# Gate and up of one transformer layer: paired 64-row products replaced by 128-row products in block 3, and by seven shared products for the last tiles of blocks 2 and 3

## The chip, the core and the metric

The kernel runs on one core of a Trainium2 chip. The time is device microseconds (us) of one execution. Five engines work side by side, each through its own queue of instructions in order: PE (TensorE, matrix products), DVE (VectorE), ACT (ScalarE), POOL (GpSimd) and SP (SyncE, which here only issues DMAs). An instruction waits on semaphores of other engines; whatever stands behind it on its own engine waits with it.

## The reference

One pre-LayerNorm layer on 2048 tokens of width 576: multi-query attention with 32 heads of width 18, then a bilinear feed-forward network (FFN) of width 4608.

```python
def _A_ref(x, wq, wk, wv, wo):            # H = 32, Dh = 18; one k and one v for all heads
    q = (x @ wq).reshape(B, S, H, Dh).transpose(0, 2, 1, 3)
    k, v = x @ wk, x @ wv
    p = softmax(einsum("bhqd,bkd->bhqk", q, k) * Dh ** -0.5)
    o = einsum("bhqk,bkd->bhqd", p, v)
    return o.transpose(0, 2, 1, 3).reshape(B, S, H * Dh) @ wo
def _B_ref(x, w_gate, w_up, w_down):
    return ((x @ w_gate) * (x @ w_up)) @ w_down
h = x + _A_ref(layernorm(x), ...)
out = h + _B_ref(layernorm(h), ...)
```

## The kernel before

The 2048 tokens are four blocks of 512 (NB = 4), the FFN width is 36 tiles of 128 (NF = 36). Every float32 operand is split into a rounded high part and a remainder, and a product is hi·hi + hi·lo + lo·hi. A split is a cast (on ACT or POOL, line L88) and a subtraction on DVE (L89).

**Gate and up.** The width 576 is nine chunks of 64 rows. For one tile the weight operand `ws` holds gate in rows 0 to 63 and up in rows 64 to 127, and `X` holds the normed tokens twice, in both halves. Each step is a pair of matmuls of 64 rows and 512 columns that work at the same time in the two halves of the array (L990). Nine chunks of three terms are 27 pairs per tile. Then ACT copies gate out of PSUM (`g`, L1020) and DVE multiplies by up (`hf`, L1024). A tile of weights (`wr`, 576 KB) is loaded by one DMA and split by POOL and DVE (128x1152).

**Down.** Two tiles together go through a scheme of seven products of quarters; its left operands are sums of quarters of the two `hf` (`S`, four DVE operations), split into the buffer `room`, and its right operands `wdo` are seven loads of 288 KB per pair of tiles from a DRAM copy made in block 0. These are 42 matmuls of 128 rows and 288 columns in 14 stages on three PSUM banks (L950, `down`). After each stage its bank is added to the residual `h`, eight times by DVE (L953), six times by an ACT copy and a POOL addition; a bank's next stage waits for that.

**Order.** The program is written out by one Python pass. Attention of the next block is interleaved with the FFN of the present one, so that the last attention work ends inside tile 24 of block 2. From there on PE has only FFN work ("gu" tiles, whose PSUM tile is `gu`), and the down products of a pair come after the first tile of the next pair. The attention output of block 3 is projected in five chunks; the last two (`project`, matmuls `yo`, L754, 24 and 16 of them) are put between these tiles by `run_aux`. When the last is added to `h`, DVE computes LayerNorm statistics (L103, L104, two BN_STATS and one BN_AGGR for each 128 tokens) and the reciprocal root (thirteen small operations, L113 to L124 and L791).

**Block 3's X.** In tile 35 of block 2 ACT makes the normed tokens `xh` (L801), PE transposes them (`tx`, 20 at L823), ACT casts, DVE subtracts, and eight DMAs from SBUF to SBUF fill X's second half (X<-X). The last pair of block 2 (48 matmuls, L908) stands between. Then block 3's 36 tiles run.

Of the kernel before, what the change touches and what calls it, by code (L numbers as in the profile page):

```python
# [25 lines left out]
P = 128  # L26
S, D, H, DH, F = 2048, 576, 32, 18, 4608
TB = 512
# [26 lines left out]
class Block:  # L55


    def __init__(self, tc, x, wq, wkv, wo, wo0, wgu, wd, cst, out):
# [3 lines left out]
        self.wgu, self.wd, self.cst, self.out = wgu, wd, cst, out  # L62
        self.pe, self.act, self.dve, self.sp = tc.nc.tensor, tc.nc.scalar, tc.nc.vector, tc.nc.sync
# [502 lines left out]
    def p_tile(self, shape, name):  # L566

        i = self.p_next = (self.p_next + 1) % (P_BUFS + (self.p2 is not None and self.n_pair >= P2_FROM))
        pool, tag = (self.pp, "P") if i < P_BUFS else (self.p2, "P2")
        return pool.tile(shape, F32, tag=tag, name=name)  # L570
# [100 lines left out]
    def chunk(self, b, c):  # L671

        if b == c == 0:
            self.oT = self.otp.tile([P, 8, TB], F32R, tag="oT", name=f"oT{b}")
        self.chunk_of(b, c)
        if b == 0 and c < 4:
            self.yos.append((c, self.project(b, c)))
            self.n_yo += 2 * NQ
        else:
            self.aux.append((self.round, lambda: drain(self.project(b, c)),  # L680
                             lambda: b in self.h and (c in self.wos and not (self.odd and (b == NB - 1 or b == 1 and c < 3)) if b else c in self.wo_in)))
# [35 lines left out]
    def load_wo_0(self, c):  # L717

        r = self.wo_r0[c] = self.w0.tile([P, D], F32, tag="wo_r", bufs=3, name=f"wo_r{c}")
        self.sp.dma_start(r, self.wo0[:, c])  # L720

    def split_wo_0(self):

        self.wo_0 = self.wp.tile([P, 2, 5, D], F32R, tag="X", bufs=1, name="wo_0")
        for c in range(3):
            if c not in self.wo_r0:
                self.load_wo_0(c)
        for c in range(5):
            self.split(self.wo_0[:, 0, c], self.wo_0[:, 1, c], self.wo_r0.pop(c), self.nc.gpsimd.tensor_copy)
            self.wo_in.add(c)  # L730
            if 0 < c < 3:
                self.load_wo_0(c + 2)
            yield
            if c == 2:
                yield

    def project(self, b, c):
# [27 lines left out]
        if c == 4:  # L765
            if b == 0:
                self.statistics(b, NQ - 1)
                self.normed[b] = self.mv, self.rstd(self.mv[:, :, 1], f"b{b}")
            else:
                last = b == NB - 1  # L770
                for i in range(4):
                    self.aux.append((self.round + i // 2, lambda i=i: self.some_statistics(b, i), self.within if last else None))
                if last:
                    self.aux.append((self.round + 2, lambda: self.scales(b), self.within))
# [7 lines left out]
    def some_statistics(self, b, s):  # L782

        self.statistics(b, s)
        if s == NQ - 1 and b < NB - 1:
            self.scales(b)
# [63 lines left out]
    def load_w(self, n):  # L850

        if n < NF * NB:
            r = self.wr[n] = self.wp.tile([P, 9, P], F32, tag="wr", bufs=2, name=f"wr{n}")
            self.sp.dma_start(r, self.wgu[n % NF])

    def split_w(self, n):
        if n < NF * NB:
# [38 lines left out]
    def down(self, b, pair):  # L896

        pe, dve, act, sp, pool = self.pe, self.dve, self.act, self.sp, self.nc.gpsimd
        h = self.h[b]
        W = [self.wdo.pop((b, pair, j), None) for j in range(7)]  # L900
        if pair == NC - 1:
            ys = {}

            def part(s, n, i):

                ms = [(self.A[:, k, 2 * i + s // 2], W[(1, 0, 2, 3)[2 * i + n]][:, l]) for k, l in ((0, 0), (0, 1), (1, 0))]
                for j, (m, k) in enumerate(ms):
                    pe.matmul(ys[s, n][:, :HD], m[:, s % 2 * P:(s % 2 + 1) * P], k, start=(i == j == 0), stop=(i == 1 and j == 2))  # L908
# [6 lines left out]
            def add(s, n):  # L915
                hs, y = h[:, s, n * HD:(n + 1) * HD], ys.pop((s, n))[:, :HD]
                if b < NB - 1 and n:
                    z = self.tmp[:, self.n_tmp % 5]
# [27 lines left out]
        for i, (t, bank, (x, w), first, (s, n), on_dve) in enumerate(STAGES):  # L946
            y = banks[bank]
            ms = [(self.A[:, k, x], W[w][:, l]) for k, l in ((0, 0), (0, 1), (1, 0))]
# [5 lines left out]
            else:  # L954
                z = self.tmp[:, self.n_tmp % 5]
# [5 lines left out]
    def room(self):  # L961
# [5 lines left out]
        self.tmp = self.hh.tile([P, 5, HD], F32, tag="tmp", bufs=1, name="tmp")  # L967
        self.n_tmp = 0

    def ffn(self, b):  # L970
        pe, act, dve = self.pe, self.act, self.dve
        X, hid, todo = self.X, [], None
        for f in range(NF):
# [11 lines left out]
            for c in range(9):  # L985
                for wk, xk in ((0, 0), (0, 1), (1, 0)):
                    if on and not last and j % 4 == 0 and self.more(b + 2):
                        self.pair()
# [25 lines left out]
            if todo and not on:  # L1014
                drain(self.down(b, *todo))
                self.more_wd(b, 7)
                self.odd = k
                self.run_aux()
# [15 lines left out]
            if f < NF - 1 and (on or not todo):  # L1034
                self.run_aux()
            todo = (f // 2,) if k else None
        if b + 1 < NB:
            both(self.spread(b + 1), self.down(b, *todo))
            self.more_wd(b + 1, WD_BUFS if b == 0 and self.first else 4)
            if b + 2 < NB:  # L1040
                self.load_x(b + 2)
        else:
            drain(self.down(b, *todo))
# [66 lines left out]

    def begin(self, first):

        self.first = first
        self.wd_list = [(b, p, j) for b in range(first, NB) for p in range(NC) for j in (range(4) if p == NC - 1 else ORDER)]
# [5 lines left out]
    def blocks(self):  # L1120
# [4 lines left out]
        self.load_w(1)  # L1125
# [30 lines left out]
        for b in range(NB):  # L1156
            self.ffn(b)
        del self.A, self.o_hl, self.S, self.tmp, self.X, self.ob, self.mv

    def run(self):  # L1160
# [3 lines left out]
        self.wd_dram = tc.dram_tile([NC, P, 7, 2, HD], F32, name="wd_dram")  # L1164
        self.m_dram = tc.dram_tile([NB, 2, H, TB], F32, name="m_dram")
        self.known, self.n_mx = [0] * NB, 0
        self.tqs, self.p2 = [], None
        self.begin(True)
        with ExitStack() as st:
# [3 lines left out]
            self.ps, self.w0 = pool("ps", 1, space=PSUM), pool("w0", 3)  # L1173
# [7 lines left out]
            with tc.tile_pool(name="p0q", bufs=1) as self.p0q:  # L1181
# [4 lines left out]
                with tc.tile_pool(name="qb", bufs=2) as self.qb:  # L1186
# [6 lines left out]
                    live, due = True, 0.0  # L1193
                    while live:
                        if self.n_pair >= WO_FROM and not self.wo_r0:
                            for c in range(3):
# [10 lines left out]
            self.wp, self.hh, self.p2 = pool("w", 2), pool("hid", 4), pool("P2", 1)  # L1207
# [17 lines left out]
P2_FROM = 240  # L1225
# [126 lines left out]
```

## Time and profile before

| what | us |
|---|---|
| median of three runs | 2279.04 |
| lowest and highest run | 2278.49, 2280.04 |
| profiled execution, its own time | 2279.61 |
| its span in the trace | 2277.8 |
| PE busy in the span | 2257.0 (99%) |
| last attention matmul to the span's end | 1813.9 to 2277.8 |

PE's matmuls overlap, so their durations add to more than their spacing; the spacing of starts tells what a step costs. The chain of waits gives, from the end backwards, which engine held the end up at each time. The end of a group in the timeline is that of its last instruction; the next group starts a little before it.

### The profile page before, as it was taken

To read this page: it belongs to the slowest core of one execution; us is meant where nothing else is said; L and a number is where in the kernel's file an instruction comes from. 1 tells how busy PE (TensorE), PEld (TensorE's weight loads), DVE (VectorE), ACT (ScalarE), POOL (GpSimd) and SP (SyncE) were. 2 spreads that over 40 slices of the span, in tenths; PEclk is the share of its full clock that TensorE was granted. 3 is DMA by queue.
4 is the path that set the end of the run, shared out by engine and by line. 5 is a ranking of instruction groups with operands and counts; after the bars stand their busy time and mean duration, and the time that the engine had idled before them with its cause. 6 is when DMAs were issued, how large, how long until landed. Compare 5 with 4: busy or idle time off the path is not lost.

```text
span 2277.8 us, 45936 instructions
## 1 busy us (share of the span) xinstructions
PE 2257.0 (99%) x18114; PEld 1618.5 (71%) x18114; DVE 1213.8 (53%) x2152; ACT 1410.2 (62%) x1832; POOL 757.7 (33%) x901
## 2 busy tenths in 40 slices
PE   8999999999999999999999999999999999999998
PEld 6433345677777777777777777777777788888897
DVE  8332436576656567444544465444445476566565
ACT  5899887766666665767666766666676533232332
POOL 4000003565555554222222232223222233333332
PEclk9999999999999999999999999999999999999999
DMA  5222314444333444534333343644333355655553
GB/s 175 75 78 72 119 31 137 151 137 143 135 126 130 143 160 137 208 115 124 114 116 107 124 132 122 194 125 123 104 122 111 121 171 177 210 172 172 182 186 109
DMA packets 127129, 306.75 MB, mean 135 GB/s; under 512 B 17553, under 2 KB 17681, under 8 KB 126265
## 3 DMA queue, kind: packets, MB, share of 16 engines
q1 hardware_dynamic: 126905, 303.73, 40.9%
q8 instruction: 145, 2.38, 0.4%
q14 instruction: 79, 0.65, 0.1%
HBM read 233.76 MB, written 55.67 MB: 127 GB/s over the span
## 4 chain that ended last, share of the span: by engine, by line
PE 95%; DVE 2%; DMA 1%; ACT 1%; issue 0%; SPq 0%; POOL 0%; DVEq 0%; ACTq 0%; POOLq 0%
PE pg L990 21%; PE acc L601 20%; PE y L950 17%; PE gu L990 13%; PE s L596 12%; PE pu L990 5%; PE yo L754 3%; PE psq L448 2%; PE y L908 1%; DMA X<-X 1%; DVE bsa L103 0%; DVE XT L89 0%; DMA x<-in_x_dram 0%; ACT P L597 0%; PE ye L908 0%
## 5 line engine op out<-in xcount | busy, mean ns | idle before, releaser
L597 ACT ACTIVATE P<-s 128x1024 f32<-128x1024 f32 x1024 | 1035.3, 1026 | 285.5 <-PE s L596 188.5
L990 PE MATMUL pu<-X,ws 64*128 64x512 f32 x2592 | 702.5, 390 | 0.1
L990 PE MATMUL pg<-X,ws 64*128 64x512 f32 x2592 | 702.4, 389 | 0.1
L990 PEld LDWEIGHTS pg<-X,ws 64*128 64x128 f32 x2592 | 479.6, 185 | 69.8 <-issue 1.2
L601 PE MATMUL acc<-P,V 128*32 128x512 f32 x4096 | 487.6, 598 | 0.0
L990 PEld LDWEIGHTS pu<-X,ws 64*128 64x128 f32 x2592 | 477.9, 186 | 13.6 <-DVE h L755 1.3
L596 PE MATMUL s<-q,kT 56*128 56x512 f32 x2048 | 448.7, 416 | 3.5 <-DVE XT L89 1.8
L950 PEld LDWEIGHTS y<-wdo,room 128*128 128x128 f32 x2856 | 386.0, 188 | 46.1 <-issue 45.8
L950 PE MATMUL y<-wdo,room 128*128 128x288 f32 x2856 | 402.1, 300 | 0.0
L957 ACT COPY tmp<-y 128x288 f32<-128x288 f32 x408 | 162.8, 399 | 329.0 <-PE y L950 313.1
L596 PEld LDWEIGHTS s<-q,kT 56*128 56x128 f32 x2048 | 211.4, 184 | 176.6 <-ACT P L597 94.7
L990 PE MATMUL gu<-X,ws 64*128 64x512 f32 x2592 | 302.0, 389 | 0.2 <-DMA X<-X 0.2
L601 PEld LDWEIGHTS acc<-P,V 128*32 128x32 f32 x4096 | 113.9, 109 | 241.5 <-issue 220.6
L990 PEld LDWEIGHTS gu<-X,ws 64*128 64x128 f32 x2592 | 251.5, 184 | 44.9 <-issue 4.8
L958 POOL TENSOR_TENSOR x<-x,tmp 128x288 f32<-128x288 f32 x204 | 158.9, 807 | 361.2 <-ACT tmp L957 360.6
L88 POOL CAST ws<-wr 128x1152 fp32r<-128x1152 f32 x144 | 171.5, 1191 | 321.0 <-PE pu L990 180.7
L958 POOL TENSOR_TENSOR h<-h,tmp 128x288 f32<-128x288 f32 x204 | 158.9, 807 | 305.8 <-ACT tmp L957 305.4
L89 DVE TENSOR_TENSOR ws<-wr,ws 128x1152 fp32r<-128x1152 f32 x144 | 219.3, 1523 | 76.1 <-POOL ws L88 76.1
L1024 DVE TENSOR_TENSOR hf<-pu,g 128x512 f32<-128x512 f32 x96 | 66.4, 691 | 358.1 <-ACT g L1020 358.0
L953 DVE TENSOR_TENSOR x<-x,y 128x288 f32<-128x288 f32 x272 | 117.5, 453 | 145.9 <-PE y L950 145.9
L953 DVE TENSOR_TENSOR h<-h,y 128x288 f32<-128x288 f32 x272 | 118.1, 455 | 111.7 <-PE y L950 108.7
L88 ACT CAST room<-hf 128x256 fp32r<-128x256 f32 (+1 forms) x144 | 73.9, 513 | 55.9 <-DVE hf L1024 55.4
(173 smaller groups left out, 1683.1 us busy)
## 6 DMA issues: line engine op xcount, KB each, us to landing
wdo<-wd_dram SPq DMA_DIRECT2D x369, 288.0 KB
wr<-in_wgu_dram SPq DMA_DIRECT2D x144, 576.0 KB
wd_dram<-wdo SPq DMA_DIRECT2D x123, 288.0 KB
q<-q_dram SPq DMA_DIRECT2D x64, 216.0 KB
raw<-in_wd_dram SPq DMA_DIRECT2D x36, 288.0 KB
q_dram<-qs SPq DMA_DIRECT2D x15, 504.0 KB
X<-X SPq DMA_DIRECT2D x24, 256.0 KB
ob<-ob SPq DMA_DIRECT2D x121, 36.0 KB
```

The source lines that it names most:

```text
L88: (copy or self.cast)(hi, src)
L89: self.dve.tensor_tensor(lo, src, f32(hi), ALU.subtract)
L596: self.pe.matmul(s_[:, i], self.kT[o:o + 56, t * P:(t + 1) * P], q[o:o + 56, pr], start=True, stop=True)
L597: self.act.activation(p_, s_, AF.Exp, scale=SCALE)
L601: self.pe.matmul(acc[32 * j:32 * j + 32, :], self.V[:, t, :], Ps[j // 2][:, j % 2, :], start=(t == 0), stop=(t == NT - 1), skip_group_chec ...
L754: pe.matmul(y[:, :HD], m, k, start=(i == 0), stop=(i == len(ms) - 1))
L950: pe.matmul(y[:, :HD], m[:, t * P:(t + 1) * P], k, start=(first and j == 0), stop=(j == 2), skip_group_check=True)
L953: dve.tensor_tensor(hs, hs, y[:, :HD], ALU.add)
L957: act.copy(z, y[:, :HD])
L958: pool.tensor_tensor(hs, hs, z, ALU.add)
L990: pe.matmul(ps, w[o:o + 64, wk, c], X[o:o + 64, xk, c], start=(j == 0), stop=(j == 26))
L1024: dve.tensor_tensor(hf, pu, g, ALU.mult)
```

## The change

Block 2 keeps its first 28 tiles (N_OLD = 100 in all). Then `two_blocks` does the rest in two stages.

1. Block 3's first 28 tiles (F1 = 28). A weight operand is one of gate and up, one half of the rows: 256 rows as two chunks of 128, and a 32-row tail. A product is seven matmuls of 512 columns: two chunks of three terms on 128 rows, and one of 96 rows that holds the three terms of the 32-row tail one under another. Four products make a tile (28 matmuls for 27 pairs): two into bank x (gate), two into bank y (up).
2. The last eight tiles of blocks 2 and 3 together: gate and up of both blocks' tokens are a two by two product of two by two halves, done in seven products of sums (49 matmuls for 54 pairs), on banks x, y and z. The sums of tokens are made once by `differences` (DVE, in the odd tiles of stage 1), the sums of weights early by `sums` (POOL, into DRAM, during the query phase).

The down products of a pair come one tile later than the next pair's first tile (a queue), and the last four pairs' down weights are loaded once for both blocks. Each weight operand is loaded as 128 rows of 256 (128 KB, eight buffers) and three DMAs of 32 rows of 128 (16 KB), and split by ACT and DVE (128x256) instead of POOL and DVE. Block 3's X is made by `transposed` (four `xh` on ACT, 16 transposes `bt` and 8 of 96 columns `btt`, four splits, two tails), with no X<-X DMAs. Smaller edits: one `wr` buffer instead of two, two early buffers for `wo_r` instead of three, more P buffers, and `run_aux(2)` once a tile in the gu tiles, which moves the two `yo` groups.

On PE, around the end of the old tiles (`yo` is the projection of block 3's attention, `gu` a tile, `y` down products, `bt` transposes). Before, the last two projections stand after y of pairs 12 and 13, and more gu tiles of block 2 follow the second:

```order
L754 MATMUL yo_4_3_0_21619<-wos_4_21373,room 128x288 x2
L754 MATMUL yo_4_3_1_21623<-wos_4_21373,room 128x288 x2
L990 MATMUL gu_21631<-X_16700,ws_21465 128x512 x54
L990 MATMUL gu_21712<-X_16700,ws_21640 128x512 x54
L950 MATMUL y_14_0_21775<-wdo_14_0_21327,room 128x288 x3
```

And after the change:

```order
L754 MATMUL yo_4_3_0_21524<-wos_4_21373,room 128x288 x2
L754 MATMUL yo_4_3_1_21528<-wos_4_21373,room 128x288 x2
L992 MATMUL gu_21536<-X_16824,ws_21465 128x512 x54
L1081 MATMUL bt_21692<-C,xh_0_21666 128x128
L1081 MATMUL bt_21692<-C,xh_1_21667 128x128
```

One gu tile (tile 27) now stands between the last projection and the transposes of block 3, where before seven gu tiles and three groups of down products stood.

On DVE at the same place, behind the additions of the last projection. Before (`hf` is a tile's hidden values, `bsb` and `mvb` the statistics of block 3):

```order
L755 TENSOR_TENSOR h_16818<-h_16818,yo_4_3_1_21623 128x288
L1024 TENSOR_TENSOR hf_21629<-gu_21454,g_21627 128x512
L89 TENSOR_TENSOR ws_21640<-wr_21392,ws_21640 128x1152
L89 TENSOR_TENSOR room<-hf_21629,room 128x256
L103 BN_STATS bsb_0_21666<-h_16818 128x6 x2
L104 BN_AGGR mvb_21665<-bsb_0_21666 128x2
L103 BN_STATS bsb_1_21670<-h_16818 128x6 x2
L104 BN_AGGR mvb_21665<-bsb_1_21670 128x2
L1024 TENSOR_TENSOR hf_21704<-gu_21631,g_21702 128x512
```

After:

```order
L1032 TENSOR_TENSOR hf_21534<-gu_21356,g_21532 128x512
L89 TENSOR_TENSOR room<-hf_21534,room 128x256
L103 BN_STATS bsb_0_21586<-h_16942 128x6 x2
L104 BN_AGGR mvb_21585<-bsb_0_21586 128x2
L103 BN_STATS bsb_1_21590<-h_16942 128x6 x2
L104 BN_AGGR mvb_21585<-bsb_1_21590 128x2
L89 TENSOR_TENSOR ws_j_21549<-wr_j,ws_j_21549 128x256 x3
L103 BN_STATS bsb_2_21631<-h_16942 128x6 x2
L104 BN_AGGR mvb_21585<-bsb_2_21631 128x2
L103 BN_STATS bsb_3_21635<-h_16942 128x6 x2
L104 BN_AGGR mvb_21585<-bsb_3_21635 128x2
L113 TENSOR_SCALAR vb_21639<-mvb_21585 128x4
```

All four groups of statistics and the thirteen small operations that begin with the last row now stand in one piece ahead of tile 27's `hf`, with three weight splits between. On ACT, at the same place after the change (the copy of tile 27's gate, the cast of its `hf`, then the normed tokens and the casts of the transposes):

```order
L1028 COPY g_21656<-gu_21536 128x512
L88 CAST room<-hf_21658 128x512
L1070 ACTIVATE xh_0_21666<-h_16942,mvb_21585,yb_21641 128x576
L1070 ACTIVATE xh_1_21667<-h_16942,mvb_21585,yb_21641 128x576
L1070 ACTIVATE xh_2_21668<-h_16942,mvb_21585,yb_21641 128x576
L1070 ACTIVATE xh_3_21669<-h_16942,mvb_21585,yb_21641 128x576
L88 CAST b_0_21670<-bt_21692 128x512
```

The normed tokens stand behind the cast of `hf` of tile 27. In the seven-product stage the end of one tile's DVE work stands so ahead of the additions of a pair's down products (`p_` and `raw_` hold products, the second L1297 is u2, L1317 is block 3's hidden values, L1324 block 2's):

```order
L1297 TENSOR_TENSOR p_24608<-p_24608,jx 128x512
L89 TENSOR_TENSOR ws_j_21549<-wr_j,ws_j_21549 128x256
L1297 TENSOR_TENSOR tail_21678<-tail_21678,jz 128x512
L1317 TENSOR_TENSOR raw_21675<-raw_21676,tail_21678 128x512
L89 TENSOR_TENSOR ws_j_21549<-wos_j,ws_j_21549 128x256
L89 TENSOR_TENSOR ws_j_21736<-wos_j,ws_j_21736 128x256
L89 TENSOR_TENSOR room<-raw_21674,room 128x512
L954 TENSOR_TENSOR h_10585<-h_10585,y_16_0_25720 128x288
L954 TENSOR_TENSOR h_10585<-h_10585,y_16_1_25721 128x288
L954 TENSOR_TENSOR h_10585<-h_10585,y_16_0_25720 128x288
L1324 TENSOR_TENSOR raw_21674<-p_24608,jx 128x512
```

The u2 addition waits for the sixth product; five operations stand between it and the first addition of the down products.

The core of the diff:

```diff
     def split_w(self, n):
-        if n < NF * NB:
+        if n < N_OLD:
...
-            self.load_w(n + 2)
+            self.load_w(n + 1)
...
     def ffn(self, b):
-        for f in range(NF):
+        for f in range(F1 if b == 2 else NF):
...
+                    if j in (8, 14, 20, 26) and not on:
+                        self.prepare(False)
+                    if n_ == N_OLD - 1 and j in (5, 20):
+                        self.first_operands(j > 5)
...
-                self.run_aux()
+                self.run_aux(2)
+                self.prepare(True)
...
+            self.two_blocks(todo[0])
...
+    def transposed(self):
...
+        for s, x in enumerate(xh):
+            act.activation(x[:, 0:D], h[:, s, :], AF.Identity, bias=mv[:, s, 0:1], scale=rs[:, s:s + 1])
+            for i in range(2):
+                pool.tensor_copy(x[:, D + 96 * i:D + 96 * i + 96].rearrange("p (t c) -> p t c", t=3),
+                                 x[:, 512 + 32 * i:544 + 32 * i].unsqueeze(1).broadcast_to([P, 3, 32]))
...
+        for c in range(4):
+            ps = (self.ps_f, self.ps_f, self.ps_m, self.ps_a)[c](f"bt{c}")
+            for s in range(NQ):
+                pe.transpose(ps[:, s * P:(s + 1) * P], xh[s][:, c * P:(c + 1) * P], self.ident)
+            self.split(self.B[c // 2][0][:, c % 2], self.B[c // 2][1][:, c % 2], ps)
...
+        for i in range(2):
+            ps = self.ps_f(f"btt{i}")
...
+    def ahead(self, tails, splits):
+        while self.n_tail < min(tails, len(SEQ)):
+            f, o = SEQ[self.n_tail]
+            for k in range(3):
+                self.sp.dma_start(f32(self.slot(self.n_tail)[32 * k:32 * k + 32, 4]),
+                                  self.t_dram[f // 9, 32 * (k // 2):32 * (k // 2) + 32, f % 9, o])
+            self.n_tail += 1
+        while self.n_split < min(splits, len(SEQ)):
+            w = self.slot(self.n_split)
+            self.split(w[:, 0:2], w[:, 2:4], self.raws[self.n_split % 8])
+            self.load_raw_operand(self.n_split + 8)
+            self.n_split += 1
+
+    def product(self, bank, n, B, first):
+        w, (hi, lo, t) = self.slot(n), B
+        ms = [(w[:, i + 2 * k], (hi, lo)[l][:, i]) for i in range(2) for k, l in ((0, 0), (0, 1), (1, 0))] + [(w[0:96, 4], t)]
+        for j, (a, m) in enumerate(ms):
+            self.pe.matmul(bank, a, m, start=(first and j == 0), stop=(j == 6), skip_group_check=True)
+
+    def refill(self, n):
+        joint = n > 4 * F1
+        self.ahead(n + (8 if joint else 6), n + (5 if joint else 4))
...
+    def two_blocks(self, pair):
...
+        for f in range(F1):
...
+            for i, (bank, B) in enumerate(((x, 0), (x, 1), (y, 0), (y, 1))):
+                self.product(bank, n, self.B[B], i % 2 == 0)
...
+        for f in range(F1, NF):
+            head = queue.pop(0) if queue else None
...
+            plan = [(x, 0, True), (y, 1, True), (x, "T2", False), (z, "T3", True), (x, "T1", False), (z, "T4", False), (x, "B22", False)]
+            for i, (bank, B, first) in enumerate(plan):
+                self.product(bank, n, self.B[B], first)
...
+                elif i == 5:
+                    add(u2, u2, z)
+                    dve.tensor_tensor(h3, p1, u2, ALU.mult)
+                self.refill(n)
+                if head and i < 3:
+                    next(head[2], None)
...
+            finish(head[:3] if head else None, lambda o=h2: dve.tensor_tensor(o, p7, x, ALU.mult))
...
+        for _ in range(2):
+            for q in queue:
+                next(q[2], None)
+        for b, p, parts, to in queue:
+            drain(self.down(b, p, to))
```

More of the change, by code (lines that the diff above doesn't have):

```diff
@@ L986, in ffn @@
                 for wk, xk in ((0, 0), (0, 1), (1, 0)):
-                    if on and not last and j % 4 == 0 and self.more(b + 2):
-                        self.pair()
+                    if on:
+                        if not last and j in SPOTS and self.more(b + 2):
+                            self.pair()
                     for o, ps in ((0, pg), (64, pu)):
@@ new lines, in slot, with first_operands @@
+    def slot(self, n):
+        first = 4 * F1
+        k = (n - first) % 8
+        return self.slots[k if n >= first and k > 5 else n % 6 if n < first else (first + k) % 6]
+    def first_operands(self, split):
+        if not split:
+            self.slots = []
+            self.more_slots()
+            self.raws = [r[:, i] for t in ("wr", "wos") for r in [self.wp.tile([P, 4, 2, P], F32, tag=t, bufs=1, name=f"{t}_j")] for i in range(4)]
+            self.n_tail = self.n_split = 0
+            for n in range(8):
+                self.load_raw_operand(n)
+            self.ahead(3, 0)
+        else:
+            self.ahead(3, 3)
@@ L1336 @@
         "wgu": wgu,
+        "wj": wj,
+        "wjt": wjt,
         "wd": wd,
```

325 lines of the change are left out of this document (286 added, 39 removed).

## The prediction, made before the changed kernel was run

> **What bounds the kernel now.** I read the page's busy times and its chain, then the chain of waits from the last attention work to the end, then PE's timeline there, then DVE and ACT at the places where the change moves things.
>
> ```profile
> PE 2257.0 (99%) x18114; PEld 1618.5 (71%) x18114; DVE 1213.8 (53%) x2152; ACT 1410.2 (62%) x1832; POOL 757.7 (33%) x901
> PE 95%; DVE 2%; DMA 1%; ACT 1%; issue 0%; SPq 0%; POOL 0%; DVEq 0%; ACTq 0%; POOLq 0%
> ```
>
> PE is the bound: what it does per step is gained or lost, and what makes it wait is added. The change lies behind 1813.86 us, where attention ends.
>
> ```profile
> 2129.77 12.46 PE gu L990 x108
> 2142.23 5.83 PE y L950 x42
> 2148.07 12.46 PE gu L990 x108
> ```
>
> In the chain of waits a pair of tiles takes 12.46 us and its down products 5.83, without a gap, so PE is limited by its own steps. Their prices come from PE's timeline (start, length, line, count).
>
> ```profile
> 1820.21 5.92 PE L950 MATMUL y<-wdo,room 128*128 128x288 f32 x42
> 1826.06 12.54 PE L990 MATMUL gu<-X,ws 64*128 64x512 f32 x108
> 1838.52 5.91 PE L950 MATMUL y<-wdo,room 128*128 128x288 f32 x42
> 1844.27 3.39 PE L754 MATMUL yo<-wos,room 128*128 128x288 f32 x24
> 1847.59 12.54 PE L990 MATMUL gu<-X,ws 64*128 64x512 f32 x108
> ...
> 1865.82 3.06 PE L754 MATMUL yo<-wos,room 128*128 128x288 f32 x16
> 1868.80 12.53 PE L990 MATMUL gu<-X,ws 64*128 64x512 f32 x108
> ...
> 1827.76 10.83 PE L990 MATMUL gu<-X,ws 64*128 64x512 f32 x94
> ...
> 33.67 3.40 PE L236 MATMUL psk<-XT,wk 128*108 128x512 f32 x14
> ...
> L236 PE MATMUL psk<-XT,wk 128*108 128x512 f32 x56 | 13.9, 398 | 0.4 <-ACT XT L88 0.4
> ```
>
> The row at 1827.76 is a window inside a group: 94 matmuls, two at a time, from the first start to the last end. Less one duration of about 0.40 us, 46 spacings are 10.43 us: 0.227 a pair. psk is the same on 128 rows, one at a time: (3.40 - 0.40) / 13 = 0.231. yo directly behind y, in the same rows, gives (3.39 - 0.30) / 23 = 0.134 for 288 columns.
>
> **The change, part by part.** *Steps.* Beyond tile 27 there were 8 + 36 tiles of 27 pairs, 1188 x 0.227 = 269.7 us. Now there are 28 x 28 + 8 x 49 = 1176 matmuls, x 0.231 = 271.6 us, every seventh on 96 rows: **+1.9**. The scheme saves 40 steps in the eight tiles, the tails add 28 in the others, and the dearer step takes the rest. The down products are the same number.
>
> *Switches between 64 and 128 rows.* From start to start y takes 1826.06 - 1820.21 = 5.85, where 42 x 0.134 = 5.64, and a pair of tiles 12.46, where 54 x 0.227 = 12.26. So each visit to the down products costs 0.21 + 0.20 = 0.41 us, and behind tile 27 there are none left. I count 22 and a half such visits before, and one and a half more at the yo groups after: 21 x 0.4 = **-8.4**. Bounds: nothing, if another gap takes their place, to -9.
>
> *The old transition of block 3.*
>
> ```profile
> 1930.09 2.62 PE L823 MATMUL tx<-C,xh 128*128 128x128 f32 x20
> 1932.47 7.16 PE L908 MATMUL y<-wdo,room 128*128 128x288 f32 x48
> 1939.56 5.73 PE L990 MATMUL gu<-X,ws 64*128 64x512 f32 x45
> 1945.44 13.71 PE L990 MATMUL gu<-X,ws 64*128 64x512 f32 x117 [0.15 <-DMA X<-X]
> 1959.07 5.91 PE L950 MATMUL y<-wdo,room 128*128 128x288 f32 x42
> ```
>
> From 1939.56 to 1959.07 81 pairs should take 18.6 with a switch and took 19.5; y took 7.09 where 48 steps and a switch are 6.65. With X<-X gone both waits go: **-1.4**. Twenty transposes take 2.38 from start to start; 24 now take 2.6 to 2.9: **+0.4**.
>
> *The new transition.* Here the biggest term lies. Before, 7 tiles and 3 groups of down products of block 2, over 60 us, stood between the last yo and tx, and they covered statistics, root and xh. Now tile 27 alone stands there. In before's time axis y of pair 11 starts at 1820.21 as now, tile 25 at 1826.06, yo of chunk 3 at 1832.4 (one tile with its switch is 6.33), tile 26 at 1835.7 (3.32, from 1844.27 to 1847.59), y of pair 12 at 1842.0, yo of chunk 4 at 1847.8, tile 27 at 1850.8 (2.98, from 1865.82 to 1868.80), and it ends at 1857.1. The DVE of before, behind the same yo, gives the durations of what must come next:
>
> ```profile
> 1866.39 3.00 DVE L755 TENSOR_TENSOR h<-h,yo 128x288 f32<-128x288 f32 x8
> 1869.31 0.68 DVE L1024 TENSOR_TENSOR hf<-gu,g 128x512 f32<-128x512 f32 x1
> 1869.91 1.35 DVE L89 TENSOR_TENSOR ws<-wr,ws 128x1152 fp32r<-128x1152 f32 x1
> 1871.17 0.42 DVE L89 TENSOR_TENSOR room<-hf,room 128x256 fp32r<-128x256 f32 x1
> 1871.50 0.82 DVE L103 BATCH_NORM_STATS2 bsb<-h 128x6 f32<-128x288 f32 x2
> ...
> 1873.28 0.21 DVE L104 BATCH_NORM_AGGREGATE mvb<-bsb 128x2 f32<-128x12 f32 x1
> ...
> 1909.08 0.16 DVE L113 TENSOR_SCALAR vb<-mvb 128x4 f32<-128x4 f32 x1
> ...
> 1911.45 0.17 DVE L791 SCALAR_TENSOR_TENSOR mvb<-mvb,yb 128x4 f32<-128x4 f32 x1
> 1924.98 0.62 ACT L88 CAST room<-hf 128x512 fp32r<-128x512 f32 x1 [1.01 <-DVE hf L1024]
> 1925.51 3.15 ACT L801 ACTIVATE xh<-h,mvb,yb 128x576 f32<-128x576 f32 x4
> ```
>
> DVE is free of yo's additions 3.5 us after yo begins: 1851.3. In its new order follow hf 0.60 (start to start), room 0.33, two groups of statistics 1.99 (1871.50 to 1873.49), three weight splits at 0.33 each, two more groups 1.99, thirteen root operations 2.54 and hf of tile 27, 0.69: 9.1 us, to 1860.4. ACT's queue holds the cast of that hf ahead of xh: 0.53 (1924.98 to 1925.51), then 3.15: 1864.2 with a handover. Only then can the 24 transposes run, 2.6 us. Their last eight reuse two banks that must be cast and subtracted first (0.62 and 0.68 from the rows above), about 0.4 more, and the tails (two ACT passes, a subtraction) make the first product wait about 0.5. So products begin at about 1867.7 and PE stands from 1857.1 for 10.6 less the transposes' own 2.6: 8, with handovers **+8.5**. Bounds: 5, if ACT passes xh sooner, to 12, if the new weights' loads hold the three splits up, behind which DVE's whole chain is queued.
>
> *A cold PE behind this pause.* The same kind of transpose at the start of the kernel, after 7.65 us without work:
>
> ```profile
> 7.65 5.15 PE L310 MATMUL warm<-C 128*128 128x128 f32 x24 [7.65 <-DMA C<-in_cst_dram]
> 12.64 1.91 PE L202 MATMUL tr<-C,xh 128*128 128x128 f32 x16
> 2272.00:2278.00 6.00, 0.00 (x0) 0.00 (x0) 0.00 (x0) 0.00 (x0) 0.00 (x0) 0.79 0.18 64
> ```
>
> 24 took 4.99 us from start to start, 0.21 each, and the next 16 0.11 each. In the last row (a window behind PE's last work at 2271; the sixth number is the granted clock) the clock has fallen to a mean of 0.79. A pause of 7 us before bt is thus likely to make its 24 transposes up to 2.5 us longer; part lies under the casts that they wait for anyway: **+1.5**, bounds 0 and 3.
>
> The Trainium skill ("TensorE: Matmul & The Clock Gate", Part 1) speaks against the change here: after an idle window of about 3.4 us the clock is halved until about 3.4 us of sustained work have passed. By it the cost would be some 1.7 us, up to double that if a second window is needed (an estimate from that page), and the sum would end at 2287 to 2289. The two slow and fast rows of transposes agree with a half clock after idling; the granted clock of that first stretch is not lower in the trace.
>
> *Inside the new stages.* In stage 1 DVE, per pair of tiles, has eight weight splits, two hf, the sums, their splits, eight additions and about four steps of `differences`, some 15 us of 18.6, and ACT less: hidden. In the seven-product tiles DVE gets the sixth product's u2 only when one product is left, 7 x 0.231 = 1.62 us. By the rows above u2 and block 3's hidden values (0.60 each), two weight splits (0.33 each) and room's 128x512 (0.60) are 2.5 us, so the first down addition starts 0.9 late. Its end, at 1.45 instead of 1.06 after the start of down (which needs that bank again after three stages of 0.40), moves the fourth stage by some 0.4. Seven pairs: **+2.8**, bounds 0 and 6. Tile 29 has no down products behind it, so tile 30's first product waits in bank x for the last multiplication: **+1.0** (0.26 behind, 0.69 its own). At the end both blocks' last pairs need four splits of 128x512 behind the additions before: **+2**, bounds 1 and 3.
>
> *SP and DMA.*
>
> ```profile
> 1817.11 0.33 SPq L854 DMA_DIRECT2D wr<-in_wgu_dram  x1
> 1818.73 6.72 SPq L668 DMA_DIRECT2D ob<-ob  x9
> 1825.56 3.37 SPq L868 DMA_DIRECT2D wdo<-wd_dram  x7
> ```
>
> SP now issues 8 loads, 24 tails and 7 wdo per pair of tiles in 18.6 us. At 0.33 each that is 12.9, at wdo's 0.48 18.7, at ob's 0.75 for the tails 25.2. The tails read DRAM as wr does, and I take 0.33 to 0.45, so SP keeps up: 0, bounds 0 and +92 (14 pairs x 6.6). `sums` adds some 60 DMAs and POOL work in the query phase, where POOL's row of the page is at 0 tenths: 0, up to +2. One wr buffer: a load has a whole tile to land: 0.
>
> *Sum*: 1.9 - 8.4 - 1.4 + 0.4 + 8.5 + 1.5 + 2.8 + 1.0 + 2.0 = +8.3 on the profiled execution's 2279.61, which lies 0.57 above the median of 2279.04: about **2287**.
>
> **The rivals.** *Not slower: the transition is covered.* If xh were ready when tile 27 ends, the terms of 8.5 and 1.5 go and the sum is -1.7: 2277. What speaks for it: PE is 99% busy before, and DVE only 53%. Against: the nine us follow from one queue's order, and xh has no way past hf of tile 27. It decides from a pause under 4.5 us, where the sum falls under the 0.2% (4.6 us) that a measurement of this kernel can tell from no change.
>
> *SP becomes the bound.* With the tails at ob's 0.75 stage 1 runs at SP's pace, +92, and the time is near 2370. For it: ob's row, the only small transfers onto few partitions in a row. Against: ob goes from SBUF to SBUF, and six products of lookahead (8 us) hide late landings.
>
> *The 96-row products are a change of mode.* If each costs 0.4 as the switch between 64 and 128 rows does, 168 of them cost +67: 2354. Against: psk after other 128-row work shows no gap, and a product of 96 rows spans more than 64. No row shows 96.
>
> *The change does what its count says and no wait is added.* Steps, switches and old waits alone: 1.9 - 8.4 - 1.4 + 0.4 = -7.5: 2271.5. It needs the pause and three DVE waits all hidden.
>
> **How the numbers follow.** Forecast 0.62 (its own range 2281 to 2294: the transition from 5 to 12, the rest of the bounds partly cancelling); covered transition 0.22, from 2273 to 2282; no wait added 0.07; SP 0.06; mode 0.03. Slower by over 0.2% (above 2283.6): most of the forecast, 0.55, with SP and mode 0.09, together 0.64. Same: 0.07 of the forecast and 0.15 of the covered case, 0.22. Faster (under 2274.5): 0.14. The range is 2273 to 2298, which leaves the two large prices and half of the last case out.
>
> **What would show it.** Right: in PE's timeline a gap of 7 to 10 us between tile 27 and bt, with DVE busy through it and ACT's xh ending it; bt at about 0.2 us a transpose; then products at 0.231 with no gap at y, 18.6 us for a pair of tiles and 17.0 plus 0.4 for a seven-product tile with its down products. Wrong: bt within 3 us of tile 27; a step of products other than 0.227 to 0.235, or a longer seventh; PE waiting for DMA or SP on ws_j in stage 1; additions of down products that hold banks up by more than 1 us.

## The result, and the profile after

Six runs of the changed kernel took 2333.8 to 2338.7 us, median 2336.12; six of the kernel before 2278.49 to 2280.04, median 2279.29. The ratio is 1.0249 (95% interval 1.0236 to 1.0262): slower by 57 us, where +8 was forecast and the range ended at 2298. The profiled execution took 2338.7, 59.1 more than that of before.

The page after, busy times and the chain by engine:

```profile
PE 2273.2 (97%) x16918; PEld 1611.0 (69%) x16918; DVE 1266.8 (54%) x2325; ACT 1462.8 (63%) x2022; POOL 778.1 (33%) x923
PE 88%; DMA 5%; DVE 4%; ACT 1%; issue 1%; SPq 1%; POOL 0%; DVEq 0%; ACTq 0%; POOLq 0%
```

The chain had 95% PE and 1% DMA; now it has 88% and 5%. PE's waits (in all us, times, longest) name what it waits for: 32-row tails of the weights, `ws_j<-t_dram`.

```profile
PE jy L1211 <- DMA ws_j<-t_dram: 21.1, 10, 5.9
...
PE y L951 <- DVE h L954: 7.5, 10, 2.4
PE bt L1081 <- ACT xh L1070: 5.9, 4, 5.1
PE jx L1211 <- DMA X<-t_dram: 2.7, 1, 2.7
```

One such wait, first in SP's timeline, then in PE's, then in the chain of waits:

```profile
2018.07 1.30 SPq L1197 DMA_DIRECT2D ws_j<-t_dram  x3
2019.46 0.37 SPq L1190 DMA_DIRECT2D wr_j<-in_wj_dram  x1
2019.93 1.30 SPq L1197 DMA_DIRECT2D ws_j<-t_dram  x3
2021.33 0.37 SPq L1190 DMA_DIRECT2D wr_j<-in_wj_dram  x1
...
2025.53 3.22 SPq L865 DMA_DIRECT2D wdo<-wd_dram  x7
2028.85 1.78 SPq L1197 DMA_DIRECT2D ws_j<-t_dram  x3
```

```profile
2031.67 1.56 PE L1211 MATMUL jy<-b,ws_j 128*128 128x512 f32 x6
2035.03 0.53 PE L1211 MATMUL jy<-tails,ws_j 96*128 96x512 f32 x1 [1.80 <-DMA ws_j<-t_dram]
2035.36 2.76 PE L1211 MATMUL jy<-b,ws_j 128*128 128x512 f32 x6
```

```profile
2025.29 3.29 PE jy L1211 x14
2029.29 0.57 SPq L1197
2029.91 4.98 DMA ws_j<-t_dram
2035.03 3.52 PE jy L1211 x8
```

SP issues without a gap in this stretch. One product's load and three tails take 1.87 us from start to start (2018.07 to 2019.93), while PE's product takes 1.62. Eight of them and seven wdo at 0.47 are 18.2 us of a pair's 18.6. When the seven wdo come in a row, the tails behind them are issued late by 3.3 us, then land 5.0 us after their issue, behind 2 MB of wdo, and PE waits. The six matmuls behind this wait take 2.76 us instead of 1.56: cold steps that follow a pause are part of its price. The granted clock shows it (a window of the changed kernel from where these steps begin; the third number from the end is the granted clock, here 0.50):

```profile
2035.30:2038.70 3.40, 3.40 (x10) 2.66 (x10) 0.00 (x0) 0.00 (x0) 0.00 (x0) 0.50 0.36 103
```

From the first product at 1874.14 to the start of the seven-product stage at 2173.64 passed 299.5 us, 39.1 more than fourteen pairs at 18.6; 31.2 of these lie between products (the PE starts' spacing above 0.231) and 7.4 inside down groups.

At the transition (PE, then DVE, then ACT of the changed kernel):

```profile
1855.96 6.42 PE L992 MATMUL gu<-X,ws 64*128 64x512 f32 x54
1867.47 0.47 PE L1081 MATMUL bt<-C,xh 128*128 128x128 f32 x1 [5.09 <-ACT xh L1070]
...
1874.14 1.97 PE L1211 MATMUL jx<-b,ws_j 128*128 128x512 f32 x6
```

```profile
1853.55 3.00 DVE L755 TENSOR_TENSOR h<-h,yo 128x288 f32<-128x288 f32 x8
...
1865.31 0.68 DVE L1032 TENSOR_TENSOR hf<-gu,g 128x512 f32<-128x512 f32 x1
```

```profile
1866.03 0.62 ACT L88 CAST room<-hf 128x512 fp32r<-128x512 f32 x1 [2.96 <-DVE hf L1032]
1866.56 3.14 ACT L1070 ACTIVATE xh<-h,mvb,yb 128x576 f32<-128x576 f32 x4
```

Tile 27 ends at 1862.4 and the first product starts at 1874.1: 11.8 us, in the order that was forecast. PE stands idle for 5.1 us of them before the first transpose, not for the 7 to 10 that the prediction gave as its sign, because the transposes begin with the first `xh` and not behind the last. Two of its signs of being wrong came: PE waits for tails in stage 1, and additions hold banks by more than 1 us.

### The profile page after: what moved, and what is told of

The parts are those of the page before. It is cut to its first block, busy times and chain, and to the rows that moved or that the text cites. A ratio compares the mean times of both kernels' runs of the same rounds, so it can differ in the third digit from the quotient of the medians.

```text
span 2336.8 us, 44958 instructions
## 1 busy us (share of the span) xinstructions
PE 2273.2 (97%) x16918; PEld 1611.0 (69%) x16918; DVE 1266.8 (54%) x2325; ACT 1462.8 (63%) x2022; POOL 778.1 (33%) x923
## 4 chain that ended last, share of the span: by engine, by line
PE 88%; DMA 5%; DVE 4%; ACT 1%; issue 1%; SPq 1%; POOL 0%; DVEq 0%; ACTq 0%; POOLq 0%
PE pg L992 20%; PE acc L601 19%; PE y L951 17%; PE s L596 12%; PE pu L992 5%; PE jx L1211 4%; PE jy L1211 4%; PE yo L754 3%; DMA ws_j<-t_dram 2%; PE psq L448 2%; PE y L909 1%; DMA wdo<-wd_dram 1%; PE gu L992 1%; SPq L1197 1%; PE jz L1211 0%
## 5 line engine op out<-in xcount | busy, mean ns | idle before, releaser
L951 PEld LDWEIGHTS y<-wdo,room 128*128 128x128 f32 x2856 | 392.7, 190 | 52.9 <-issue 38.4
L951 PE MATMUL y<-wdo,room 128*128 128x288 f32 x2856 | 408.9, 302 | 7.6 <-DVE h L954 7.5
L89 DVE TENSOR_TENSOR ws<-wr,ws 128x1152 fp32r<-128x1152 f32 x100 | 161.4, 1614 | 80.5 <-POOL ws L88 80.5
L88 POOL CAST ws<-wr 128x1152 fp32r<-128x1152 f32 x100 | 121.3, 1213 | 245.7 <-PE pu L992 159.8
L1211 PE MATMUL jy<-b,ws_j 128*128 128x512 f32 x372 | 100.9, 409 | 0.0
L1211 PE MATMUL jx<-b,ws_j 128*128 128x512 f32 x372 | 97.0, 396 | 0.0
L89 DVE TENSOR_TENSOR room<-S,room 128x1024 fp32r<-128x1024 f32 x68 | 87.5, 1287 | 15.5 <-ACT room L88 15.4
```

Source lines behind the costliest of these rows:

```text
L88: (copy or self.cast)(hi, src)
L89: self.dve.tensor_tensor(lo, src, f32(hi), ALU.subtract)
L951: pe.matmul(y[:, :HD], m[:, t * P:(t + 1) * P], k, start=(first and j == 0), stop=(j == 2), skip_group_check=True)
L1211: self.pe.matmul(bank, a, m, start=(first and j == 0), stop=(j == 6), skip_group_check=True)
```

## The experiments

Theory A: SP's queue is full, and the tails stand behind its issue rate. Rival B: the tails land late behind the burst of wdo's bytes. The other runs take the terms that PE's spacing shows beside them: the pause at the transition, late additions in both stages, the cold PE.

**One DMA per tail.**

```diff
-            for k in range(3):
-                self.sp.dma_start(f32(self.slot(self.n_tail)[32 * k:32 * k + 32, 4]),
-                                  self.t_dram[f // 9, 32 * (k // 2):32 * (k // 2) + 32, f % 9, o])
+            self.sp.dma_start(f32(self.slot(self.n_tail)[0:96, 4]), self.t_dram[f // 9, :, f % 9, o])
...
-            for k, src in enumerate((hi, r)):
+            for k, src in enumerate((hi, hi, r)):
```

> The tails of one weight operand come in one DMA of 96 rows instead of three of 32 (same bytes and rows into SBUF; DRAM holds the high parts twice, for which the query phase stores 20 DMAs more). SP then issues 2 DMAs per product, not 4: by the trace after, 0.47 us each, 0.94 instead of 1.87 us per product, against PE's 1.62. Theory A, SP's issue rate is what delays the tails: PE's waits on ws_j<-t_dram (21 us in the trace after) and nearly all of the 31 us lost between products of stage 1 go, some 4 us of the seven-product stage too; time 2298 to 2304. Rival B, the tails are late because they land behind the burst of seven wdo loads (5 us each in the trace): the burst stays, at most a third is won back, time above 2320.

Measured: 2303.5 (2302.69 to 2304.58), ratio 1.0106 (1.0089 to 1.0123), 32.6 us less. SP now has gaps even around the burst:

```profile
1979.83 0.34 SPq L1190 DMA_DIRECT2D wos_j<-in_wj_dram  x1
1980.26 0.38 SPq L1196 DMA_DIRECT2D ws_j<-t_dram  x1
1981.36 0.34 SPq L1190 DMA_DIRECT2D wr_j<-in_wj_dram  x1
...
1986.79 6.20 SPq L865 DMA_DIRECT2D wdo<-wd_dram  x7
```

No wait of PE on a tail is left, stage 1 takes 270.6 us instead of 299.5, and PE's excess between products falls from 31.2 to 1.7. The seven wdo still stand in a row ahead of the tails, so B as it was stated, with at most a third won back, falls. They are less dense, though: SP is now ahead of its work and issues them over 6.2 us instead of 3.2. Whether seven loads issued as densely as before would still make a tail land late was not tried by itself.

**wdo loads spread, one per product.** The count of DMAs stays.

```diff
-                self.load_wd(self.n_wd + 7)
+                self.wd_due += 7
...
     def refill(self, n):
+        if self.wd_due:
+            self.wd_due -= 1
+            self.load_wd(self.n_wd + 1)
```

> The seven wdo loads behind a pair's down products are issued one per product instead of seven in a row; the count of SP's DMAs is the same. Theory A (SP's issue rate: 8 x 1.87 + 7 x 0.47 = 18.3 us of 18.6 a pair): SP is as full as before, little changes, 2325 to 2340. Rival B (tails wait behind the burst, in SP's queue for 3.3 us and in the DMA engines for some 5): the waits go for the most part, 2300 to 2312.

Measured: 2308.48 (one run). Stage 1 takes 271.3 us, and PE waits on tails once, 0.5 us, and twice on wdo, 2.1 in all.

```profile
1998.26 1.31 SPq L1197 DMA_DIRECT2D ws_j<-t_dram  x3
1999.66 0.37 SPq L1190 DMA_DIRECT2D wos_j<-in_wj_dram  x1
2000.08 0.43 SPq L865 DMA_DIRECT2D wdo<-wd_dram  x1
2000.61 1.30 SPq L1197 DMA_DIRECT2D ws_j<-t_dram  x3
```

SP issues as many DMAs as ever, and nearly all of PE's waits on tails are gone: A alone falls too.

**Both remedies.** The two diffs above together.

> One DMA per tail and the wdo loads one per product: both remedies at once. If rate and burst were two separate losses their gains would add (32 and 28 us: 2275). If the loss needs both, a queue without slack and a burst in it, either remedy takes it all and the second adds nothing: 2300 to 2305, with PE's waits on tails at zero.

Measured: 2305.57 (one run), as with either. So the gains don't add, and the loss is one thing that needs both: a queue with no slack, in which a burst of seven makes the tails late and which then has no room to catch up before the next burst.

**The tails on ACT's queue.**

```diff
-                self.sp.dma_start(f32(self.slot(self.n_tail)[32 * k:32 * k + 32, 4]),
+                self.act.dma_start(f32(self.slot(self.n_tail)[32 * k:32 * k + 32, 4]),
```

> The three tail DMAs of an operand are issued from ACT's queue instead of SP's; number, size and rows stay. Theory A (SP's issue rate): SP has 1 DMA per product and the wdo loads left, the tails no longer stand behind them, and the waits of PE on tails go: 2298 to 2306, unless ACT's own work is held up by issuing. Rival B (landing behind wdo's bytes in the DMA engines): issue moves but landings stay near 5 us, at most 15 us won. Rival C (512-byte rows are slow in the DMA engines themselves): no change, 2330 to 2340.

Measured: 2382.83 (one run), which none of the three expected. PE has no wait on tails among its eight largest in the two stages; these lead instead (all in us, times, longest):

```profile
PE y L951 <- DVE h L954: 37.2, 19, 3.0
PE jy L1211 <- DVE hf L1281: 13.6, 13, 2.0
```

The issues, which wait for free slots, stand in ACT's queue ahead of the casts and copies that DVE and the down groups need, as here in ACT's timeline, where a cast stands 3.30 us behind them:

```profile
2111.61 1.26 ACTq L1197 DMA_DIRECT2D ws_j<-t_dram  x3
2112.91 0.41 ACT L88 CAST ws_j<-wos_j 128x256 fp32r<-128x256 f32 x1 [3.30 <-issue]
```

The tails are no longer late, but the cost of issuing them only changed engines, and there it was worse.

**Thirty tiles instead of 28** (F1 = 30), on top of one DMA per tail.

> As the kernel with one DMA per tail, but with block 2 keeping 30 tiles and block 3 having 30 in 128-row products, six shared. Two more gu tiles and a group of down products then stand between the last projection and the transposes. Transition theory: the pause of 8 to 9 us at bt and the cold transposes (1.5) go; it costs ten steps (2.3 us), one more visit of the down products among 64-row work (0.4), and saves one pair of late down additions (about 1): 6 to 9 us faster than the kernel with one DMA per tail. Rival: the pause comes from something else that moves along (weight loads, ACT): no faster, 2 to 3 us slower.

Measured: 2300.4 (2298.9 to 2309.32), ratio 1.0104 (1.0083 to 1.0125); by the medians 3 less than the kernel with one DMA per tail, but the intervals overlap, so the verdict rests on the trace:

```profile
1875.51 1.91 PE L1081 MATMUL bt<-C,xh 128*128 128x128 f32 x16
1877.35 6.43 PE L992 MATMUL gu<-X,ws 64*128 64x512 f32 x54
1883.71 1.08 PE L1087 MATMUL btt<-C,xh 128*96 128x128 f32 x8
```

The pause is gone and the transposes run at 0.11 us each between gu tiles. The rest of the gain went back at once: the two down groups ahead of it are held by DVE for 2.7 and 2.8 us, where the one in the kernel with 28 tiles lost 2.0.

**differences() in two steps per odd tile.**

```diff
-                else:
+                elif i < 2:
                     next(work, None)
```

> One DMA per tail, and differences() takes two steps in each odd tile of stage 1, behind its first two products, instead of four; its 27 steps then fill 14 odd tiles instead of 7. Theory: of the late down additions of stage 1 in the kernel with one DMA per tail (8.8 us in all, 1.9 in each of three pairs, 2.2 in a fourth, 0.6 to 0.7 in the first two) nearly all comes from the 1.2 us steps that stand ahead of the additions on DVE: 5.5 to 7.5 us faster than that kernel's 2303.5, so 2296 to 2298. Rival: the lateness comes from the weight splits there, and more tiles get a share of it: no gain, 2301 to 2306.

Measured: 2297.66 (2296.93 to 2303.49), ratio 1.0082 (1.0068 to 1.0096). With four steps, in the changed kernel, DVE's queue runs so into the down additions:

```profile
1927.53 1.22 DVE L1102 TENSOR_TENSOR t<-raw,X 128x1024 fp32r<-128x1024 f32 x1
1928.67 0.81 DVE L954 TENSOR_TENSOR h<-h,y 128x288 f32<-128x288 f32 x2
```

The additions begin 2.4 us after their group's first matmul (1926.3). With two steps, the excess inside stage 1's down groups falls from 8.8 to 2.3 us, about 0.15 in each, and the stage from 270.6 to 263.9 us. The theory held.

**Part four of the left operands three products earlier**, in the shared tiles.

```diff
-                if head and i < 3:
+                if head and i < 4:
```

> One DMA per tail, and in a seven-product tile the fourth part of the left operands (cast and subtraction of 128x512) comes behind the fourth product instead of just ahead of the down products. Theory: the 0.7 us by which each of six down groups is held in the seven-product stage is DVE's work behind the sixth product; without this 0.60 us it shrinks to 0.15 each: 2 to 4 us faster than 2303.5, with 1 us more from the first such tile at the most. Rival: the additions wait for the last weight splits (their casts on ACT), no gain, within 1 us.

Measured: 2300.34 (2299.35 to 2301.55), ratio 1.0092 (1.0078 to 1.0106). The same down group, first in the kernel with one DMA per tail, then here:

```profile
2204.52 4.85 PE L951 MATMUL y<-wdo,room 128*128 128x288 f32 x33 [0.32 <-DVE h L954]
```

```profile
2203.05 5.92 PE L951 MATMUL y<-wdo,room 128*128 128x288 f32 x42
```

The group is no longer broken after nine matmuls; what each takes above 42 steps falls from 0.72 to about 0.15 us (a group without any wait has that too) and the shared stage, up to its last groups, from 130.6 to 128.3 us. Of the 3.4 us that the six groups won a third came back between the products (11.6 us for this tile's 49 instead of 11.4). The theory held.

**Idle transposes in the pause.**

```diff
+        idle = self.ps_a("idle")
+        for i in range(64):
+            pe.transpose(idle[:, i % 4 * P:(i % 4 + 1) * P], self.ident, self.ident)
```

> The kernel with one DMA per tail, with 64 idle transposes of the identity put on PE between tile 27 and the transposes of block 3, about as long (7.2 us) as PE waits there. Nothing reads them. Theory of a cold PE: the stretch from the first full-speed chance of bt to the first product shrinks, the 21 transposes behind the last xh (4.3 us in the kernel with one DMA per tail) take 2.4 to 3.2 and the first product begins 1 to 2 us sooner behind tile 27's end than the 11.8 us there. Rival: the transposes wait for the casts and subtractions anyway, first product within 0.5 us of 11.8.

Measured: 2304.51 (one run; the down group ahead was late by 4.3 us here, by 2.0 in the kernel it is set against, with a pause of 2.4 instead of 1.7 us and, behind it, a granted clock of 0.50 for 3.41 us). PE's timeline of that kernel, then of this one:

```profile
1868.42 3.03 PE L1081 MATMUL bt<-C,xh 128*128 128x128 f32 x13 [0.28 <-ACT xh L1070]
1871.25 1.68 PE L1087 MATMUL btt<-C,xh 128*96 128x128 f32 x8
1872.69 1.65 PE L1209 MATMUL jx<-b,ws_j 128*128 128x512 f32 x6
```

```profile
1871.15 2.02 PE L1084 MATMUL bt<-C,xh 128*128 128x128 f32 x16
1873.36 1.15 PE L1090 MATMUL btt<-C,xh 128*96 128x128 f32 x8 [0.18 <-DVE b L89]
1874.27 1.64 PE L1212 MATMUL jx<-b,ws_j 128*128 128x512 f32 x6
```

Cold, 21 transposes took 4.3 us up to the first product; kept busy, PE did all 24 in 3.1, at 0.12 each. From tile 27's end to the first product are 10.1 us instead of 11.6 in the kernel it is set against (the 11.8 is the changed kernel's): the cold PE cost 1.5 us, by the trace of this place.

**All remedies with 30 tiles**: one DMA per tail, wdo spread, two steps, part four earlier, F1 = 30.

> All remedies together: one DMA per tail, wdo loads one per product, two steps of differences() per odd tile, the fourth part earlier, and 30 tiles instead of 28 in the old and the 128-row form. Theory: from the 2300.4 of the kernel with 30 tiles, 6 to 7 us less for the late additions of stage 1 and 2 for five down groups of the shared stage: 2290 to 2293, still slower than before by what is left: late additions beside the moved projections (5.6 us there), the last pair (2), the early part (1 to 2), a dearer step. Rival: the late additions reappear elsewhere: 2297 to 2301.

Measured: 2294.52 (2291.57 to 2299.72), ratio 1.0068 (1.0054 to 1.0082), 1.5 to 4.5 above what was expected. Both stages kept their gains (2.4 us left in all down groups of stage 1), but the two groups beside the moved projections lost 4.2 and 4.0 us instead of 2.7 and 2.8. Their waits are the same as in the kernel with one DMA per tail and 30 tiles; what differs is the clock. The rest of the first group there, then here, and a window of this kernel behind the wait (the third number from the end is again the granted clock):

```profile
1847.10 4.67 PE L951 MATMUL y<-wdo,room 128*128 128x288 f32 x33 [2.39 <-DVE h L954]
```

```profile
1848.36 6.18 PE L951 MATMUL y<-wdo,room 128*128 128x288 f32 x33 [2.39 <-DVE h L954]
```

```profile
1849.40:1852.70 3.30, 3.30 (x16) 3.30 (x15) 0.57 (x2) 1.56 (x4) 2.32 (x3) 0.50 0.50 124
```

So some 2.7 us of this execution are no lateness of DVE but a halved clock behind two pauses, which the other execution was spared.

**The projections back in their old places, 32 tiles**, on top of all remedies.

```diff
-... and not (self.odd and self.more(NB) and (b == NB - 1 or b == 1 and c < 3)) ...
+... and not (self.odd and (b == NB - 1 or b == 1 and c < 3)) ...
```

> All remedies, with the last two projections back behind the down products of pairs 12 and 13 as before the change, and 32 tiles instead of 30 in the old and the 128-row form so that statistics, root and xh stay covered. Theory: the late additions of the two down groups there (8.4 us in the kernel with all remedies and 30 tiles, where DVE has a projection's eight additions just ahead) fall to under 1 us; two more tiles cost ten steps (2.3) and one more visit (0.4); 4 to 6 us faster than that kernel's 2294.5, so 2288 to 2291. Rival: the lateness there comes from the other DVE work that the transition brings and moves along: 2295 to 2298.

Measured: 2294.23 (2292.55 to 2296.0), ratio 1.0062 (1.0048 to 1.0076): no gain. The groups of pairs 12 and 13 now lose 1.0 and 0.8 us, but that of pair 14, behind root, hf and weight splits, loses 2.7. Each side had half of it. The group of pair 14 shows the same two waits (0.73 and 1.30 us) as that of pair 13 in the kernels with 30 tiles, so this lateness comes from the transition's own DVE work and moved along with it. The 2.7 that the group of pair 12 lost there at a full clock came with the moved projections. In all three groups the move won 1 us against that kernel, less than the 2.7 that two more tiles were forecast to cost. The last pairs' groups took 3.9 us above their steps instead of 2.0; that is no lateness that moved, for their waits are nearly the same, and the granted clock was 0.50 from 2273.3 to 2276.7. No version that was run beats the kernel before.

## Why the prediction was wrong, point by point

**The step that failed is "SP and DMA"**, which was put at 0 with a bound of +92. It had the count right (8 loads, 24 tails, 7 wdo) and its own line at wdo's 0.48 us gave 18.7 us of 18.6, but it then took 0.33 to 0.45 for the small DMAs from the one row of wr, though a row of wdo stood beside it. Tails and loads cost 0.47 from start to start. It also treated SP as a rate only: that seven wdo stand in a row ahead of the tails, and that a queue at 98% can't catch up, was not in it. One DMA per tail gave back 32.6 of the 57 us. "Six products of lookahead (8 us) hide late landings" was the argument against the rival (six at 1.62 are 9.7). Where SP keeps up, the changed kernel's tails are indeed issued 9 us ahead of their product (at 2035.22 for the one that starts at 2044.29), but behind the burst shown above 2.8 (2028.85 for 2031.67), less than the 5.0 that the landing took. The chance of 0.06 for a full SP, and its single price of +92, were the two mistakes.

**Mis-sized terms.** "Steps" and "Switches" were put at -6.5 together, and that was too good by 5 to 6 us. A pair of stage 1 without late additions takes 18.8 us (thinned-out steps) and a shared tile with its down products 17.3 (part four earlier), where two tiles and a group took 18.3 before: fourteen times 0.5 lost and eight times 1.0 won leave 1 us. The step is 0.233 rather than 0.231, and a down group takes 5.8 rather than 5.63. So even with every wait gone there was hardly anything to win.

"Inside the new stages ... stage 1 hidden" was wrong by some 6 us (8.8 in down groups, 2.3 with the steps thinned out): DVE's 15 us of 18.6 is a sum over the pair, and the 1.2 us steps stood just ahead of the additions. In the shared stage +2.8 was put for seven groups held 0.4 each; six of them took 0.72 above their steps, of which 0.15 is no wait, and 1.6 in the first two of the changed kernel. Tile 30's wait was 1.0 and measured 1.3 in the kernel with one DMA per tail; the last pair 2.0 and 2.0.

**Terms that were missing.** Attention ended 2.4 us later in the profile (the first gu tile starts at 1816.28, not 1813.86); 0.4 of it is the wait for the very first load, the rest was not traced to a cause. And the group of pair 12 lost 2.7 us (2.6 more than before), because the projection moved ahead of it puts eight additions and then tile 26's work on DVE:

```profile
1835.53 3.28 DVE L755 TENSOR_TENSOR h<-h,yo 128x288 f32<-128x288 f32 x8 [1.75 <-PE yo L754]
...
1847.94 0.81 DVE L954 TENSOR_TENSOR h<-h,y 128x288 f32<-128x288 f32 x2
```

y of pair 12 had begun at 1844.59. The prediction followed that move on PE alone, where it costs one switch.

**What held.** The transition: hf of tile 27 was put at 1860.4 and came at 1865.3, of which 2.4 us are the late start and 2.5 the late group ahead of it; 10.6 us of pause plus 1.5 of cold transposes were forecast, 11.8 measured in all. The cold price of 1.5 was confirmed by the idle transposes. The Trainium skill's rule for it ("TensorE: Matmul & The Clock Gate", Part 1, a halved clock after an idle window) agrees with the transposes. That the granted clock was not lower in the kernel's first stretch, as the prediction says, tells nothing: the trace's record of it begins only at 12.44 us, where the transposes go from 0.21 to 0.11. Inside stage 1 the measurement differs from the Trainium skill's idle window of 3.4 us, since shorter pauses did it: of the five tail waits that put 1.9 us or more between two steps, four (2.0, 3.0, 3.1 and 6.1 us) were followed by steps of 0.43 us instead of 0.23, and one of 2.8 us was not. In the trace of the changed kernel every change of the granted clock lies on one grid of 3.41 us; the pause of the 2.8 fell on both sides of a grid line (1.1 us and 1.5), that of the 2.0 inside one interval. The forecast reckoned with a cold PE at the transition alone. The 96-row products cost 0.23 like the others, so that rival is dead. The five differences add up: 2.4 for the start, 2.6 for pair 12, -0.3 for the transition, 39.1 in stage 1 and a remainder of 7.0 for the shared stage and the end are 50.8 beyond the forecast's 8.3, together the 59.1 of the profile. The 39.1 themselves, by the stage's length in the kernels that take one cause away after the other, are 28.9 for SP (299.5 to 270.6), 6.7 for the steps of `differences` (to 263.9) and 3.5 for the dearer pair.

## What to carry to other kernels

When a change turns few large DMAs into many small ones, count the issuing queue's time like an engine's, at the dearest row of its kind; above some nine tenths, look for the bursts in its order, because lateness in a full queue stays. Merging the small ones or thinning out the burst each sufficed here, and moving the issues to an engine that has other work cost more than it saved. On an engine that is half idle the place of an operation still counts: what stands just ahead of a down group's additions is paid, and the same operation a few products earlier costs far less. And where two versions wait alike but differ by a microsecond or two, compare the granted clock behind the waits before looking for a cause in the queues.

## What the runs showed of the hardware that was not expected

A DVE operation can take several times its length while POOL works. In one execution of the kernel with the thinned-out steps PE lost some 7 us in the query phase, beginning here (DVE, then POOL):

```profile
147.66 3.87 DVE L88 CAST oT<-ob 126x512 fp32r<-126x512 f32 x1 [5.55 <-DMA ob<-ob]
```

```profile
146.66 4.58 POOL L1419 TENSOR_TENSOR sums<-sums 128x2048 fp32r<-128x2048 f32 x1
```

The median of the five such casts is 0.43; this one ends 0.3 us after POOL's long subtraction of `sums`. At 1839.90 in the changed kernel a 128x256 subtraction took 1.28 us instead of 0.42, while POOL cast `ws`. The Trainium skill ("SBUF — State Buffer", Who interferes with whom) says that DVE and GpSimd share one pair of SBUF ports as an exclusive lock held for a whole instruction; both numbers agree. Whether this explains why the changed kernels' times scatter more than those of before (2296.9 to 2303.5 against 2278.5 to 2280.1) was not tried. The granted clock has a share in it: the five runs with all remedies and 30 tiles took 2291.6 and 2292.4 us at a mean clock of 0.999, and 2294.5, 2295.7 and 2299.7 at 0.998, 0.997 and 0.996. Pauses like the one above set it down: there it was 0.50 for 6.8 us from 152.9.
